# Half steps of 18-wide attention, spread over each segment of a recurrence

## The chip, the cores and the metric

The kernel runs on one core of one Trainium2 chip. TensorE multiplies matrices into PSUM; ScalarE, VectorE and POOL work beside it, each on its own list of instructions in a fixed order; SP and POOL issue transfers. The metric is the device time of one launch in microseconds, the median of the runs shown.

## The reference

Two attentions over the same `x` (2048 x 576) are mixed by a gate:

```python
def _A_ref(x, mem0, Wq, Wk, Wv, Wo, seg_len):      # H = 32 heads of 128, M = 8, seg_len = 32
    mem = mem0
    for s in range(n_seg):                          # 64 segments, one after the other
        h = concatenate([mem, xs], axis=1)          # 8 + 32 = 40 rows
        q, k, v = h @ Wq, h @ Wk, h @ Wv            # 576 -> 32 heads x 128
        p = softmax(where(mask, q k^T * scale, -1e9))
        o = (p v) Wo
        mem = o[:, :M, :]                           # carried to the next segment
        outs.append(o[:, M:, :])

def _B_ref(x, wqkv, wo):                            # 32 heads of 18, all 2048 rows, no mask
    ...
    p = softmax(q k^T * scale)
    return (p v) @ wo

return g * a + (1 - g) * b                          # g = sigmoid(sum(x * gate_w))
```

## The kernel before, in words

A first part (to about 270 us) transposes `x`, projects q, k and v of the 18-wide attention B for all rows into DRAM (`qtd`, `ktd`, `vgd`, four heads per group of 32 rows each, the rows beyond 18 being zero), and projects ahead the last 8 rows of every segment of A. Then the recurrence A runs through its 64 segments, and B is laid into it as filler. A last part mixes both and writes the output.

One step of B is one block of 128 keys against 512 queries, for the four heads of a group: four score matmuls `sb` (L330; two heads share one tile of two PSUM banks, and there are two such tiles), two exponentials `etb` on ScalarE (L342) and four matmuls of values `ob` (L346). There are 8 groups x 4 query blocks x 16 key blocks = 512 steps, written as a generator `b_steps` that `b_advance(k)` moves on by k steps. After 16 steps VectorE turns and divides `ob` (L360 to L371) and SP stores it. A new group loads `qtg`, `ktg` and `vgi` on POOL's queue into single buffers.

One segment of A: `project` (L449) multiplies the 32 rows in `ht` with half of wq, wk or wv, twenty matmuls of 512 columns, four at a time in four column strips of the array; VectorE copies the result to `tm` (L474). `turn` (L462, L465) transposes q and k with eight matmuls each into `qt` and `kt`; v goes by four transfers from `tm` into `v_sb` (L480). Then, for two halves `b` of the heads: `psh` scores (L490), exponential `et` (L498), mask by a minimum (L500); and again for two halves: sums `pss` (L508), reciprocals `rq`, broadcast `prb` (L518), product (L526), values `pso` (L531), copy to `ot` (L539). The output projection `pbw` (L547) is 160 matmuls of 128 rows, 128 columns and 40 moving columns; its first 8 columns go into the next segment's `ht` (L558 to L560).

The code writes 8 steps of B behind each segment. A scheduler decides each engine's order from the dependences and the order in the code, when the kernel is built; the lists are then fixed. Before, it moves most of the steps of one segment into the next one's first projections and softmax, seven or nine of them per segment; none stand within `pbw`. The names `sb`, `ob`, `etb` belong to B, the others to A.

## Time and profile before

| what | value |
|---|---|
| median of 3 runs | 2172.97 us (2172.16 to 2174.61) |
| the profiled execution | 2173.49 us, span 2171.8 us |
| mean granted TensorE clock | 0.857 |
| TensorE busy | 1924.1 us, 89% |
| ScalarE busy | 1087.5 us, 50% |
| VectorE busy | 822.1 us, 38% |
| DMA, mean | 54 GB/s |

A line of groups reads: line, engine, operation, output and inputs, shapes, count, busy time and mean ns of one, then the idle time of its engine ahead of it and what ended that. A line of the timeline reads: start, length, engine, line, operation and count; lengths of matmuls are those of records that overlap one another, so what one costs is read from start to start. A line of stretches gives the busy time of each engine between two points of the span, and the clock that TensorE was granted in it.

### The profile page before, as it was taken

The page shows a single profiled execution, that of the slowest core. Times are in us where ns is not written, and L with a number is a line of the kernel's source. Part 1 is how long each engine was busy: PE and PEld are TensorE (multiplying, and loading weights), DVE is VectorE, ACT ScalarE, POOL GpSimd, SP SyncE. Part 2 cuts the span into 40 slices and gives each one's busy share as a digit, 9 for nine tenths or more (in the row PEclk, how much of TensorE's full clock was granted, in tenths as well). Part 3 has the DMA queues.
Part 4 walks back from the last instruction along what each step waited for, and adds up shares of the span by engine and source line. Part 5 has one row for each costly group of instructions (what it writes and reads, how often), then busy time and mean ns, then how long its engine had stood idle before and what let it go on. Part 6 is the DMA issues. An engine that isn't in the chain of part 4 may idle for free.

```text
span 2171.8 us, 67407 instructions
## 1 busy us (share of the span) xinstructions
PE 1924.1 (89%) x30629; PEld 1083.2 (50%) x30646; DVE 822.1 (38%) x1867; ACT 1087.5 (50%) x1282; POOL 106.4 (5%) x268
## 2 busy tenths in 40 slices
PE   4799979998999899989998999989998999899986
PEld 2358735554455455554454555555544555455443
DVE  4223323333333333443433333334343333333444
ACT  2122255555555555546555555545555555555540
POOL 3000000000000000000000000000000000000000
PEclk8899978888888888888888888888888888888889
DMA  8553240001000100010001000010001000100015
GB/s 257 227 139 110 119 157 25 24 25 53 24 24 24 47 25 24 25 50 28 21 27 40 25 25 24 26 53 25 24 25 48 21 24 25 53 21 21 24 43 153
DMA packets 110291, 117.27 MB, mean 54 GB/s; under 512 B 56108, under 2 KB 91636, under 8 KB 106932
## 3 DMA queue, kind: packets, MB, share of 16 engines
q1 hardware_dynamic: 85652, 90.50, 13.4%
q10 hardware_dynamic: 20896, 9.87, 1.9%
q0 software_dynamic: 3456, 12.58, 1.8%
q8 instruction: 240, 3.93, 0.7%
q14 instruction: 47, 0.39, 0.1%
HBM read 58.91 MB, written 37.22 MB: 44 GB/s over the span
## 4 chain that ended last, share of the span: by engine, by line
PE 58%; ACT 23%; issue 7%; DMA 7%; DVE 4%; SPq 1%; ACTq 0%; POOL 0%; DVEq 0%
ACT etb L342 21%; PE pbw L547 15%; PE pvv L449 11%; PE sb L330 7%; PE ob L346 5%; PE pq L284 3%; PE pso L531 3%; PE pq L218 3%; PE prb L518 3%; PE pt L462 2%; DMA v_sb<-tm 2%; PE pq L268 2%; PE pss L508 1%; DVE et L526 1%; DMA otn<-otd 1%
## 5 line engine op out<-in xcount | busy, mean ns | idle before, releaser
L342 ACT ACTIVATE etb<-sb 128x1024 bf16<-128x1024 f32 x1024 | 990.1, 1027 | 813.9 <-PE sb L330 806.3
L474 DVE CAST tm<-pvv 128x512 bf16<-128x512 f32 x384 | 265.7, 692 | 530.3 <-PE pvv L449 530.3
L330 PE MATMUL sb<-qtg,ktg 18*128 18x512 bf16 x2048 | 404.4, 428 | 44.4 <-ACT etb L342 29.9
L547 PE MATMUL pbw<-ot,wo 128*128 128x40 bf16 x10240 | 326.6, 195 | 0.8 <-issue 0.8
L547 PEld LDWEIGHTS <-wo 128*128 128x128 bf16 x10240 | 320.0, 108 | 4.1 <-issue 0.9
L346 PE MATMUL ob<-etb,vgi 128*32 128x512 bf16 x2048 | 246.5, 425 | 53.7 <-ACT etb L342 43.1
L449 PEld LDWEIGHTS <-ht 128*32 128x32 bf16 x7680 | 185.5, 96 | 213.1 <-issue 70.9
L449 PE MATMUL pvv<-wq_m,ht 128*32 128x512 bf16 x2048 | 205.3, 388 | 0.0
L330 PEld LDWEIGHTS <-ktg 18*128 18x128 bf16 x2048 | 90.1, 92 | 223.7 <-issue 198.6
L346 PEld LDWEIGHTS <-vgi 128*32 128x32 bf16 x2048 | 95.2, 95 | 188.0 <-issue 158.3
L449 PE MATMUL pvv<-wk_m,ht 128*32 128x512 bf16 x2048 | 169.2, 380 | 0.0
L539 DVE CAST ot<-pso 128x320 bf16<-128x320 f32 x256 | 114.4, 487 | 91.8 <-PE pso L531 91.7
L449 PE MATMUL pvv<-wv_m,ht 128*32 128x512 bf16 x2048 | 133.3, 380 | 0.0
L558 DVE CAST ht<-pbw 128x32 bf16<-128x32 f32 x63 | 12.1, 192 | 271.1 <-PE pbw L547 271.1
L531 PEld LDWEIGHTS <-v_sb 64*128 64x128 bf16 x2048 | 65.3, 105 | 71.0 <-issue 57.3
L526 DVE TENSOR_TENSOR et<-et,prb 128x320 bf16<-128x320 bf16 x128 | 62.3, 487 | 97.0 <-PE prb L518 97.0
L418 POOL COPY ht<-xg 128x144 bf16<-128x144 bf16 x64 | 19.8, 310 | 1567.7 <-PE pvv L449 1567.7
L531 PE MATMUL pso<-et,v_sb 64*128 64x40 bf16 x2048 | 75.6, 196 | 23.6 <-DVE et L526 12.0
L218 PE MATMUL pq<-xT,wpk 128*128 128x512 bf16 x313 | 76.4, 405 | 18.4 <-ACT stg L228 16.1
L500 DVE TENSOR_TENSOR et<-et,cap 128x320 bf16<-128x320 bf16 x128 | 42.3, 331 | 122.0 <-ACT et L498 121.9
L490 PE MATMUL psh<-qt,kt 128*64 128x40 bf16 x2048 | 56.9, 189 | 33.6 <-DVE kt L465 33.6
L518 PE MATMUL prb<-ident,rq 128*64 128x128 bf16 (+1 forms) x768 | 71.5, 272 | 16.3 <-DVE rq L514 16.3
(103 smaller groups left out, 1524.5 us busy)
## 6 DMA issues: line engine op xcount, KB each, us to landing
v_sb<-tm SPq DMA_DIRECT2D x256, 64.0 KB
wo<-in_A_Wo_dram SPq DMA_DIRECT2D x4, 1152.0 KB
wv_m<-in_A_Wv_dram SPq DMA_DIRECT2D x4, 1024.0 KB
wq_m<-in_A_Wq_dram SPq DMA_DIRECT2D x4, 1024.0 KB
wk_m<-in_A_Wk_dram SPq DMA_DIRECT2D x4, 1024.0 KB
qtd<-stg SPq DMA_DIRECT2D x8, 512.0 KB
ktd<-stg SPq DMA_DIRECT2D x8, 512.0 KB
vgd<-vt ACTq DMA_DIRECT2D x16, 256.0 KB
```

The source lines that it names most:

```text
L218: nc.tensor.matmul(pq[:, :], lhsT=wpk[:, c, :, :].rearrange("p j e -> p (j e)"), rhs=xT[:, c, t * QC:(t + 1) * QC], start=(c == 0), stop=( ...
L284: nc.tensor.matmul(pv[:, o:o + P], lhsT=lw, rhs=xL[:, cc, q * P:(q + 1) * P], start=(c == 0), stop=(c == NF),)
L330: nc.tensor.matmul(sb[:, i, :], lhsT=ktg[32 * j:32 * j + DhB, kb * P:(kb + 1) * P], rhs=qtg[32 * j:32 * j + DhB, qc * QC:(qc + 1) * QC], s ...
L342: nc.scalar.activation(out=etb[:, :, :], in_=sbs[jp][:, :, :], func=ACT.Exp, scale=scale_b)
L346: mm = nc.tensor.matmul(ob[32 * j:32 * j + 32, :], lhsT=vg[:, kb * P + 32 * j:kb * P + 32 * j + 32], rhs=ets[j // 2][:, j % 2, :], start=( ...
L449: nc.tensor.matmul(pv[32 * j:32 * j + 32, :], lhsT=ht[:, cc, :], rhs=rw, start=(c == 0), stop=(c == NF), tile_position=(0, 32 * j),)
L474: nc.vector.tensor_copy(out=tm[:, hf * 512:(hf + 1) * 512], in_=pv[:, :])
L518: nc.tensor.matmul(prb[64 * jj:64 * jj + 64, o:o + n], lhsT=rq[0:n, 2 * k + jj:2 * k + jj + 1].to_broadcast([n, 64]), rhs=ident[0:n, 0:n], ...
L526: nc.vector.tensor_tensor(out=et[:, b, :], in0=et[:, b, :], in1=prb[:, 0:W8], op=ALU.mult)
L531: nc.tensor.matmul(pso[:, i * L:(i + 1) * L], lhsT=v_sb[64 * jj:64 * jj + 64, b * 1024 + i * Dh:b * 1024 + (i + 1) * Dh], rhs=et[64 * jj:6 ...
L539: nc.vector.tensor_copy(out=ot[:, j * HG:(j + 1) * HG, :].rearrange("p h t -> p (h t)"), in_=pso[:, 0:W8])
L547: nc.tensor.matmul(pbw[:, c * L:(c + 1) * L], lhsT=wo[:, h, d0:d0 + P], rhs=ot[:, h, :], start=(h == heads[0] and c == 0), stop=(h == head ...
```

## The change

A step of B is cut in two. A half step computes the two scores and the exponential of one pair of heads; the values of the block before are multiplied behind the first half (`values(kb - 1, before)`), so that they come one half step or more after their exponentials. The score operands take all 32 rows of a head's strip instead of 18; the added rows are zero. The 1024 half steps are given out by `tick`, sixteen times per segment (after each of the six projections, after each half of the scores, after the product and after the values of each half, and four times within the output projection), each time 0.98 of a half step on average. v is projected in two parts cut by half `b`, the first ahead of `psh`, the second behind it; each part needs four transfers of half the width.

```diff
-                for kb in range(NKB):
-                    sbs = []
...
-                                lhsT=ktg[32 * j:32 * j + DhB, kb * P:(kb + 1) * P],
-                                rhs=qtg[32 * j:32 * j + DhB, qc * QC:(qc + 1) * QC],
...
+                before = None
+                for kb in range(NKB):
+                    ets = []
+                    for jp in range(2):
+                        sb = ps_bs.tile([P, 2, QC], FP32, name="sb")
+                        for i in range(2):
+                            j = 2 * jp + i
+                            nc.tensor.matmul(
+                                sb[:, i, :],
+                                lhsT=ktg[32 * j:32 * j + 32, kb * P:(kb + 1) * P],
+                                rhs=qtg[32 * j:32 * j + 32, qc * QC:(qc + 1) * QC],
...
+                        etb = bint3.tile([P, 2, QC], BF16, name="etb")
+                        nc.scalar.activation(out=etb[:, :, :], in_=sb[:, :, :], func=ACT.Exp, scale=scale_b)
+                        ets.append(etb)
+                        if jp == 0 and before is not None:
+                            values(kb - 1, before)
+                        yield
+                    before = ets
+                values(NKB - 1, before)
...
-    per_seg = int(round(total_steps / (n_seg + 1)))
+    pace = [0.0]
+    per_tick = total_steps / (n_seg + 1) / 16
+
+    def tick():
+        pace[0] += per_tick
+        k = int(pace[0])
+        pace[0] -= k
+        b_advance(k)
...
+            tm = seg2.tile([P, 512], BF16, name="tm", bufs=6)
+            nc.vector.tensor_copy(out=tm[:, :], in_=pv[:, :])
+            tick()
+            return tm
...
+        def project_v(b):
+
+            tm = project(wv, [(2 * jj + b) * 1024 + u * 512 for jj in range(2) for u in range(2)])
+            for jj in range(2):
+                for u in range(2):
+                    nc.sync.dma_start(
+                        out=v_sb[64 * jj:64 * jj + CT, b * 1024 + u * 512:b * 1024 + (u + 1) * 512],
+                        in_=tm[64 * jj + 32 * u:64 * jj + 32 * u + CT, :],
+                    )
+
+        tq2 = [project(wq, [j * 1024 + hf * 512 for j in range(4)]) for hf in range(2)]
+        tk2 = [project(wk, [j * 1024 + hf * 512 for j in range(4)]) for hf in range(2)]
+        turn(tq2, qt)
+        turn(tk2, kt3)
+        project_v(0)
...
+            tick()
+        project_v(1)
...
+            if heads.index(h) % 8 == 7:
+                tick()
...
-        b_advance(per_seg)
```

What the built order makes of it, at three places. First TensorE at the end of an output projection before: its last matmul, values and scores of B, all 160 matmuls of `pbw` having gone ahead of them.

```order
L547 LDWEIGHTS wo
L547 MATMUL pbw<-ot,wo 128x40
L346 LDWEIGHTS vgi
L346 MATMUL ob<-etb,vgi 32x512
L330 LDWEIGHTS ktg
L330 MATMUL sb<-qtg,ktg 128x512
```

The same engine a quarter into an output projection of the changed kernel:

```order
L569 LDWEIGHTS wo
L569 MATMUL pbw<-ot,wo 128x40
L347 LDWEIGHTS ktg
L347 MATMUL sb<-qtg,ktg 128x512 [waits Activation_49]
L347 LDWEIGHTS ktg
L347 MATMUL sb<-qtg,ktg 128x512
L328 LDWEIGHTS vgi
L328 MATMUL ob<-etb,vgi 32x512 [waits Activation_49]
```

Forty matmuls of `pbw` now stand between a pair of scores and the next, and values of B follow every second pair.

Second, ScalarE around the two exponentials `et` of one segment's own scores, before:

```order
L342 ACTIVATE etb_20373<-sb_20368 128x1024
L342 ACTIVATE etb_20837<-sb_20831 128x1024
L342 ACTIVATE etb_20839<-sb_20834 128x1024
L498 ACTIVATE et_2858<-psh_20549 128x320
L498 ACTIVATE et_2858<-psh_20568 128x320
L342 ACTIVATE etb_20867<-sb_20861 128x1024
L342 ACTIVATE etb_20869<-sb_20864 128x1024
```

and changed:

```order
L356 ACTIVATE etb_20722<-sb_20719 128x1024
L516 ACTIVATE et_2858<-psh_20728 128x320
L356 ACTIVATE etb_20750<-sb_20747 128x1024
L516 ACTIVATE et_2858<-psh_20756 128x320
L356 ACTIVATE etb_20778<-sb_20775 128x1024
L356 ACTIVATE etb_20806<-sb_20803 128x1024
L356 ACTIVATE etb_20834<-sb_20831 128x1024
```

Before, five exponentials of B go ahead of both `et` in a row; now one `etb` stands between the two, and TensorE has the scores of `psh` in pieces around a pair.

Third, SP's queue over one segment, before (v in four transfers from one `tm`, between the loads of rows projected ahead):

```order
L480 DMA v_sb_2856<-tm_21068 32x1024 x4
L438 DMA xl_22079<-qld_85 128x256
L438 DMA xl_22082<-kld_86 128x256
L432 DMA v_sb_2856<-vld_84 8x2048 x2
L416 DMA xg_24873<-xtd_79 128x768
L480 DMA v_sb_2856<-tm_21622 32x1024 x4
```

and changed:

```order
L492 DMA v_sb_2856<-tm_20155 32x512 x4
L451 DMA xl_21135<-qld_85 128x256
L451 DMA xl_21138<-kld_86 128x256
L492 DMA v_sb_2856<-tm_20239 32x512 x4
L445 DMA v_sb_2856<-vld_84 8x2048 x2
L492 DMA v_sb_2856<-tm_20717 32x512 x4
```

v now leaves in two groups of four, and the loads of `xl` for the next segment stand between them.

## The prediction

> **What bounds the kernel now.** I read the page first, then the stretches of single segments, then the order of instructions inside one segment, and last the granted clock in short steps.

> ```profile
> PE 1924.1 (89%) x30629; PEld 1083.2 (50%) x30646; DVE 822.1 (38%) x1867; ACT 1087.5 (50%) x1282; POOL 106.4 (5%) x268
> L342 ACT ACTIVATE etb<-sb 128x1024 bf16<-128x1024 f32 x1024 | 990.1, 1027 | 813.9 <-PE sb L330 806.3
> ...
> PE psh L490 <- DVE kt L465: 33.6, 64, 0.5
> PE sb L330 <- ACT etb L342: 29.9, 89, 1.2
> PE pso L531 <- DMA v_sb<-tm: 9.7, 7, 2.4
> ```

> TensorE is busy for 89% of the span; ScalarE, whose exponentials (L342) take 990.1/1024 = 0.97 us each, is half idle. The three rows of waits show that little of TensorE's time is idle in the trace's own sense. Next come stretches from one write of the new memory into `ht` (L558) to the next: 62 segments together, then four single ones.

> ```profile
> 315.10:2091.57 1776.47, 1613.29 (x27480) 891.34 (x27479) 684.63 (x1628) 992.34 (x1116) 76.78 (x206) 0.85 0.10 29
> ...
> 1005.09:1033.93 28.84, 26.49 (x451) 14.27 (x450) 11.77 (x28) 17.85 (x20) 1.05 (x3) 0.88 0.11 30
> 1033.93:1060.59 26.66, 24.61 (x438) 13.84 (x434) 9.98 (x25) 14.03 (x16) 1.06 (x3) 0.87 0.08 19
> 1060.59:1090.37 29.78, 27.51 (x451) 14.72 (x450) 11.77 (x29) 17.96 (x20) 1.06 (x3) 0.83 0.08 22
> ...
> 1173.45:1203.56 30.11, 24.21 (x435) 13.98 (x434) 12.22 (x29) 13.97 (x16) 2.74 (x6) 0.83 0.25 74
> ```

> Behind the length stand the busy times of TensorE, its weight loads, VectorE, ScalarE and POOL, then the granted clock, the DMA share and GB/s. A segment costs 1776.47/62 = 28.65 us, and 64 of them make the time. The first and third hold the same work (17.9 us of ScalarE, nine 18-wide steps) and differ only in clock, 0.88 against 0.83. Where that clock goes, the next rows show, in steps of 3.41 us:

> ```profile
> 1017.99:1021.40 3.41, 2.71 (x58) 1.63 (x51) 1.58 (x3) 1.82 (x2) 0.69 (x3) 1.00 0.29 85
> 1021.40:1024.81 3.41, 2.68 (x24) 1.05 (x24) 2.89 (x9) 3.11 (x6) 0.37 (x2) 1.00 0.33 88
> 1024.81:1028.23 3.42, 3.34 (x37) 1.54 (x35) 1.49 (x6) 2.46 (x3) 0.00 (x0) 0.50 0.14 43
> 1028.23:1031.64 3.41, 3.37 (x96) 3.11 (x94) 1.18 (x3) 1.94 (x2) 0.00 (x0) 0.50 0.06 19
> 1031.64:1035.05 3.41, 3.41 (x106) 2.57 (x104) 0.85 (x4) 0.46 (x1) 0.00 (x0) 1.00 0.02 5
> ...
> 284.12:287.53 3.41, 3.41 (x24) 0.74 (x26) 0.00 (x0) 2.32 (x4) 0.00 (x0) 0.50 1.08 390
> 287.53:290.95 3.42, 3.42 (x34) 0.97 (x26) 0.69 (x1) 2.14 (x3) 0.00 (x0) 0.50 1.09 392
> 290.95:294.36 3.41, 3.13 (x40) 1.03 (x36) 0.69 (x1) 3.40 (x4) 0.00 (x0) 1.00 0.67 225
> ```

> **The change, part by part.** The costs of single visits on TensorE at full clock (second column: us):

> ```profile
> 1012.48 0.39 PE L346 MATMUL ob<-etb,vgi 128*32 128x512 bf16 x4
> 1012.80 0.39 PE L330 MATMUL sb<-qtg,ktg 18*128 18x512 bf16 x2
> 1013.12 0.83 PE L449 MATMUL pvv<-wk_m,ht 128*32 128x512 bf16 x11
> ...
> 1014.30 0.40 PE L346 MATMUL ob<-etb,vgi 128*32 128x512 bf16 x4
> 1014.52 1.04 PE L449 MATMUL pvv<-wk_m,ht 128*32 128x512 bf16 x14
> ...
> 1016.26 1.05 PE L449 MATMUL pvv<-wv_m,ht 128*32 128x512 bf16 x16
> 1018.54 0.62 PE L462 MATMUL pt<-ident,tm 128*128 128x128 bf16 x8
> ...
> 1020.01 0.89 PE L490 MATMUL psh<-qt,kt 128*64 128x40 bf16 x32 [0.53 <-DVE kt L465]
> 1020.83 0.39 PE L330 MATMUL sb<-qtg,ktg 18*128 18x512 bf16 x2
> ...
> 1049.88 0.32 PE L508 MATMUL pss<-bsel,et 128*128 128x2 bf16 x3
> 1050.48 0.45 PE L518 MATMUL prb<-ident,rq 128*64 128x128 bf16 x6 [0.28 <-DVE rq L514]
> 1050.86 0.39 PE L330 MATMUL sb<-qtg,ktg 18*128 18x512 bf16 x2
> 1051.51 0.48 PE L531 MATMUL pso<-et,v_sb 64*128 64x40 bf16 x16 [0.27 <-DVE et L526]
> 1051.92 0.33 PE L508 MATMUL pss<-bsel,et 128*128 128x2 bf16 x3
> ```

> From start to start: two projections 1016.26 to 1018.54, so 1.14 each; eight transposes 0.55; `psh` x32 0.82; a pair of scores 0.32; values ahead of a projection 0.22 (1014.30 to 1014.52), ahead of another kind 0.32 (1012.48); `prb` 0.38; `pso` x16 0.41, taken as 0.5; `pss` about 0.3. Sums to their broadcast (`pss` to `prb`, through VectorE) take 0.60, broadcast to `pso` 1.03. Then the output projection, the exponential's delay, and one VectorE step at the end of a query block:

> ```profile
> 1032.00:1033.80 1.80, 1.80 (x76) 1.79 (x72) 1.00 0.05 9
> 1056.00:1058.00 2.00, 2.00 (x66) 2.00 (x63) 0.50 0.16 41
> ...
> 1005.31 0.39 PE L330 MATMUL sb<-qtg,ktg 18*128 18x512 bf16 x4
> 1005.74 8.51 ACT L342 ACTIVATE etb<-sb 128x1024 bf16<-128x1024 f32 x9 [5.98 <-PE sb L330]
> 1006.81 0.40 PE L346 MATMUL ob<-etb,vgi 128*32 128x512 bf16 x4 [0.36 <-ACT etb L342]
> ...
> L364 DVE TENSOR_TENSOR tn<-tq,rtb 128x512 bf16<-128x512 f32 x32 | 22.4, 700 | 1.1
> ```

> Records of 0.195 us overlap the ends of a stretch, so a `pbw` matmul takes (1.80 + 0.195)/76 = 0.026 us at full clock and 0.033 at half. From the start of a score pair to the values that need its exponential: 1.50 us; exponentials in a row: 8.51/9 = 0.95.

> Now one segment of the changed order, at full clock, on TensorE:
> 1. Four projections (q, q, k, k) with four score pairs and two visits of values: 4 x 1.14 + 4 x 0.32 + 2 x 0.22 = 6.3; sixteen transposes 1.1. Sum 7.4. No exponential is late: pairs stand 1.5 us apart.
> 2. First half of v 1.14, `psh` in three pieces 0.82 + 0.2, four score pairs 1.3, values 0.33, second half of v 1.14: 4.95. The wait for `kt` (33.6 us in all) is gone, since v's first half lies over VectorE's two copies. The second v half covers the exponentials of `psh`.
> 3. The softmax: work of five score pairs, three visits of values, two each of `pss`, `prb`, `pso`, about 5.0; and three waits. Values wait 0.3: the exponential of the pair ahead of v's second half queues behind `psh`'s two and ends 0.6 into this stretch, behind a pair of 0.32. The first `pso` waits 0.3: 1.03 less `prb` and a pair. Later a pair at 3.75 has its values no earlier than 5.25, where a pair and `prb` end at 4.5: 0.75. Behind the waiting values stands the chain's own `pso`, so all three are paid: 6.35.
> 4. Output projection 160 x 0.026 = 4.2, four switches 0.4, four pairs 1.3, two values 0.65: 6.5. The copies to `ht` lie under the last pair and values.

> That is 25.2 us. What comes on top: the transposes of every fourth segment 0.1; VectorE's four instructions at the end of a query block, of 0.70 us each (L364), one of them in the chain's way in a third of the segments, 0.2; the seven changes of head group, 3.4 us each in the rows (30.11 against 26.66 with equal ScalarE time), 0.35 per segment, kept as it is, since a new group's first scores still wait for its loads. So 25.85 without the clock, against 28.65 - 2.5 = 26.15 before. The spreading takes away waits for exponentials and the clump of scores, and pays in visits: the orders have 2112 and 2650 changes between kinds of matmul with different rows and columns of the array. Each costs 0.32 - 0.22 = 0.1 us by the rows above; 538 more are 54 us, already in the walk.

> [...] Were it the whole rest of a record (0.39 - 0.22 = 0.17 us), the sum would be 37 us higher; the rows show 0.1.

> The clock: stretch 3 is as thin as the step at 1021.40 (4 visits of 512 columns and short matmuls per 3.41 us), and at 6.35 us it is nearly two grid steps long, so a step falls inside it in every segment and the clock still halves. It should return in the output projection, which now follows at once: mostly two steps (6.8 us), at times three or one; I take 7.2 us, at 0.29 us each 2.1. Segment: 27.95, and 28.65 - 27.95 = 0.7 us x 64 = 45 us gained. The end loses some 2 us, because the last score steps now run beside the last segment and their values are turned and stored after it. 2173.5 (the profiled execution; the median of the three runs shown is 2173.0) - 45 + 2 = 2130 us.

> Bounds: stretch 3 lies between its work alone, 5.0, and 7.8 (every wait twice as long); half clock between one step (1.0 us) and three (3.0). Edits that I cost at nothing: scores with 32 rows, since 18-row and 128-row matmuls of 512 columns have the same 0.39 us above (a gain is excluded too: columns set the time); score tiles allocated one by one, with two buffers as before; POOL's copy into the next `ht`, which waits for the last projection as before and is needed a segment later. The v transfers double from four to eight per segment, and this row prices the four:

> ```profile
> 1019.46 2.42 SPq L480 DMA_DIRECT2D v_sb<-tm  x4
> ```

> 0.6 us of issue each: the first half's are out 3 us ahead of its `pso`; the second half's stand behind the two loads of `xl` in SP's queue (which nobody needs before the next segment) and are out some 1.3 us ahead. Where the queue was late before, TensorE waited (9.7 us in 7 times). Cover gone costs 0.5 us per segment, 32 us; I take 0.

> **Rivals.**
> *The clock stays low through the output projection.* At half clock the new mixture (40 `pbw`, a pair, 40 `pbw`, a pair, values) has a third of its time in pairs that fill little of the array. Before, `pbw` in a block brought the clock back in the steady part; at the start, a step with 24 matmul records of projections, scores and values did not (284.12), one with 34 did (287.53, then 1.00). If the mixture falls short, half clock lasts into the next segment's projections: some 4 us of softmax, 9 of output projection (160 x 0.033 and six visits of 0.55), 2.5 of projection, 15.5 us: 8.3 x 0.29 = 2.4 us x 64, 2130 + 154 = 2284. It decides if the mixture, a third of whose time is pairs, counts for less than a step like that at 287.53.
> *The clock never drops.* [...] With the thin stretch filled by pairs and values, the step at 1021.40 might no longer occur: 2130 - 2.1 x 64 = 1996. Against it: five pairs and three visits of values in 6.35 us are no denser than what stood there before.
> *The spread buys nothing.* Exponentials and v transfers become the wait in stretch 3, where eight pairs stand within 8 us (7.6 us of exponentials, and those of `psh`): 0.6 to 1.2 us more per segment, 2168 to 2207. For it: ScalarE was busy 3.11 of 3.41 us there before. Against it: it is idle elsewhere, and no queue builds up. That the spread isn't there is excluded by the order above.

> **Numbers.** Forecast 0.51 (its own range 2070 to 2168), clock low longer 0.20, clock never low 0.07, nothing bought 0.22. No change means within 0.2%, 4 us, about what a measurement tells: 0.05, from the last case, which leaves 0.17 of it slower. Faster 0.58, slower 0.37. The range 2060 to 2275 leaves out the full-clock case and half of the low-clock one.

> **What would show it.** After: a mean segment near 28.0 us with ScalarE near 16 us in every one instead of 14 and 18; `psh` without a wait for `kt`; one low stretch of the clock per segment, of two grid steps, ending inside the `pbw` rows; waits of `pso` on `et` and of `ob` on exponentials of 0.3 to 0.8 us. A clock under 0.8 over the segments, or waits of `pso` on `v_sb` in most of them, would make the forecast wrong.

## Result and the profile after

The changed kernel takes 2076.5 us (median of 4 runs, 2072.8 to 2082.6) against 2172.6 us of the kernel before: a ratio of 0.956 [0.954, 0.959], 96 us less. The prediction was 2130 us: the direction was right and the time lies within the range, but the gain is more than twice the 43 us forecast. One execution of one kernel below, the one with all three edits together, took 2273.1 us at a mean clock of 0.648; its figures are those of the other three.

The page of the changed kernel, rows of engines and granted clock, and from the groups the exponentials:

```profile
PE 1929.8 (93%) x30629; PEld 1081.4 (52%) x30646; DVE 831.7 (40%) x1867; ACT 1119.7 (54%) x1282; POOL 107.0 (5%) x268
PEclk9899988888888888888888899888889988888999
...
L356 ACT ACTIVATE etb<-sb 128x1024 bf16<-128x1024 f32 x1024 | 1029.9, 1026 | 690.4 <-PE sb L347 689.2
```

TensorE is busy for as long as before (1924.1 us), so nearly all that went is time in which it stood still; the clock is only a little higher (0.874 against 0.857 in the profiled executions). Stretches, with the same columns as before: 62 segments from first projection to first projection, then two single segments.

```profile
318.73:1991.54 1672.81, 1610.64 (x27423) 887.57 (x27425) 693.64 (x1629) 1009.82 (x1102) 77.42 (x206) 0.87 0.11 31
1105.82:1132.73 26.91, 26.02 (x442) 14.55 (x434) 9.68 (x22) 16.45 (x18) 1.05 (x3) 0.81 0.07 19
1216.92:1242.30 25.38, 25.13 (x443) 13.82 (x443) 9.97 (x25) 16.52 (x19) 1.05 (x3) 0.93 0.08 20
```

A segment costs 1672.81/62 = 26.98 us instead of 28.65, and ScalarE has 1009.82/62 = 16.3 us in it. Not in every one, as the prediction's last paragraph had it: in about half of the segments it is within 0.2 us of 16.5, in the others it lies between 13.6 and 18.5; before, it was 13.2 to 15.0 or 16.9 to 19.0. TensorE's waits:

```profile
PE ob L328 <- ACT etb L356: 21.8, 43, 0.6
...
PE sb L347 <- DMA ktg<-ktd: 11.2, 4, 7.1
...
PE pso L552 <- DVE et L546: 8.0, 25, 0.9
...
PE pso L552 <- DMA v_sb<-tm: 5.9, 15, 0.9
PE sb L347 <- ACT etb L356: 4.9, 13, 1.2
...
PE psh L508 <- DVE kt L483: 0.2, 1, 0.2
```

The wait for `kt` is gone (33.6 us before), and the waits for exponentials and for `et` are 21.8 + 8.0 + 4.9 = 34.7 us in 81 places, half a microsecond per segment. In the kernel before they were 85.0 us in 227 places: the 29.9 for `sb` that the prediction shows, and these two:

```profile
PE ob L346 <- ACT etb L342: 43.1, 114, 0.7
...
PE pso L531 <- DVE et L526: 12.0, 24, 1.0
```

The segment at 1105.82 of the changed kernel shows such waits, in the order of TensorE's work in its softmax:

```profile
1119.91 0.39 PE L347 MATMUL sb<-qtg,ktg 32*128 32x512 bf16 x2
1120.56 0.48 PE L552 MATMUL pso<-et,v_sb 64*128 64x40 bf16 x16 [0.26 <-DVE et L546]
1120.97 0.40 PE L328 MATMUL ob<-etb,vgi 128*32 128x512 bf16 x4
...
1121.98 0.45 PE L538 MATMUL prb<-ident,rq 128*64 128x128 bf16 x6
1123.06 0.61 PE L328 MATMUL ob<-etb,vgi 128*32 128x512 bf16 x3 [0.63 <-ACT etb L356]
```

and the segment at 1216.92 has none in the same places, because its values stand elsewhere among the half steps:

```profile
1230.57 0.45 PE L538 MATMUL prb<-ident,rq 128*64 128x128 bf16 x6
1231.12 0.40 PE L328 MATMUL ob<-etb,vgi 128*32 128x512 bf16 x4
1231.45 0.39 PE L347 MATMUL sb<-qtg,ktg 32*128 32x512 bf16 x1
1231.76 0.49 PE L552 MATMUL pso<-et,v_sb 64*128 64x40 bf16 x16
...
1233.20 0.45 PE L538 MATMUL prb<-ident,rq 128*64 128x128 bf16 x6
1233.68 0.40 PE L328 MATMUL ob<-etb,vgi 128*32 128x512 bf16 x4
1234.01 0.39 PE L347 MATMUL sb<-qtg,ktg 32*128 32x512 bf16 x2
1234.33 0.56 PE L552 MATMUL pso<-et,v_sb 64*128 64x40 bf16 x16
```

The clock in its 3.41-us steps, through the segment at 1105.82:

```profile
1112.07:1115.49 3.42, 3.42 (x62) 2.07 (x60) 2.48 (x4) 1.48 (x2) 0.00 (x0) 1.00 0.00 0
1115.49:1118.90 3.41, 3.41 (x51) 1.49 (x50) 1.18 (x3) 3.21 (x6) 1.05 (x3) 1.00 0.16 42
1118.90:1122.31 3.41, 3.15 (x50) 1.86 (x46) 1.91 (x8) 3.02 (x4) 0.00 (x0) 1.00 0.22 60
1122.31:1125.73 3.42, 2.79 (x54) 1.85 (x55) 1.38 (x3) 1.61 (x2) 0.00 (x0) 0.50 0.12 37
1125.73:1129.14 3.41, 3.41 (x62) 2.05 (x59) 0.00 (x0) 1.35 (x2) 0.00 (x0) 0.50 0.02 5
1129.14:1132.55 3.41, 3.41 (x86) 2.88 (x82) 0.00 (x0) 1.72 (x2) 0.00 (x0) 0.50 0.00 0
```

It halves behind the softmax's step, as before, and here returns after the third step, at the end of the output projection. Of the 62 segments 28 have two steps at half clock, 19 three, 11 one, two four and two none.

Stages tell more than one segment. Each row of this table is a mean over the 62 segments of one profiled execution: the stages run from the first `pvv` of q to the first `pt`, to the first `psh`, to the first `pss`, to the first `pbw`, and to the next segment. "Half" is the time at half clock, (1 - mean clock) x 2 x segment, with the clock of the stretch in hundredths, so good to some 0.3 us; "at full" is the segment less 0.3 us for each us at half clock, a price that the prediction took as 0.29 and that the last experiments give as 0.33 to 0.35. In the text a score pair is two score matmuls of B, a visit of values the four matmuls `ob` of one step.

| kernel | time us | segment | project | turn, v | pairs | softmax | out | half | at full |
|---|---|---|---|---|---|---|---|---|---|
| before | 2172.6 | 28.65 | 9.59 | 4.30 | 2.27 | 6.54 | 5.95 | 8.6 | 26.1 |
| before, 32 rows | 2164.6 | 28.54 | 9.59 | 4.30 | 2.27 | 6.46 | 5.92 | 8.0 | 26.1 |
| whole steps at the end | 2132.1 | 27.86 | 10.35 | 2.78 | 2.36 | 6.43 | 5.94 | 5.6 | 26.2 |
| half steps at the end | 2119.6 | 27.61 | 10.11 | 2.86 | 2.33 | 6.62 | 5.70 | 5.0 | 26.1 |
| **changed** | 2076.5 | 26.98 | 6.53 | 2.68 | 3.81 | 5.91 | 8.06 | 7.0 | 24.9 |
| changed, 18 rows | 2101.2 | 27.31 | 6.66 | 2.68 | 3.82 | 5.92 | 8.22 | 8.2 | 24.9 |
| changed, v together | 2095.8 | 27.31 | 6.52 | 4.30 | 1.95 | 6.44 | 8.11 | 9.3 | 24.5 |
| changed, whole steps | 2126.5 | 27.75 | 6.69 | 3.00 | 3.92 | 6.25 | 7.90 | 6.7 | 25.8 |
| none in `pbw` | 2060.4 | 26.74 | 7.98 | 3.12 | 3.80 | 6.02 | 5.82 | 5.4 | 25.1 |
| none in `pbw`, half of it early | 2005.8 | 25.79 | 8.01 | 3.12 | 3.80 | 3.99 | 6.87 | 3.1 | 24.9 |
| changed, two buffers | 2055.9 | 26.60 | 6.45 | 2.68 | 3.83 | 5.72 | 7.92 | 6.9 | 24.5 |
| changed, values later | 1988.1 | 25.46 | 6.47 | 2.68 | 3.62 | 5.80 | 6.87 | 3.6 | 24.4 |
| changed, 4 matmuls added | 2117.0 | 27.63 | 6.56 | 2.68 | 3.85 | 6.57 | 7.97 | 6.6 | 25.6 |
| changed, 8 matmuls added | 2039.1 | 26.31 | 6.64 | 2.68 | 3.81 | 6.18 | 7.01 | 1.1 | 26.0 |
| early half and two buffers | 1979.9 | 25.44 | 8.06 | 3.12 | 3.82 | 3.75 | 6.69 | 2.5 | 24.7 |
| these and values later | 1913.1 | 24.22 | 7.73 | 2.72 | 3.60 | 3.96 | 6.21 | 1.0 | 23.9 |

Before to changed, TensorE's idle time ahead of its matmuls falls from 2.64 to 1.00 us per segment, which is nearly the whole 1.67: 0.70 to 0.03 in the projections, 0.92 to 0.02 in the two stages from the turns to the first `pss` (the `kt` wait and exponentials), 0.94 to 0.78 in the softmax. The stages change by more than that, because work of B moved between them. The projections lose 3.06 us: they hold 3.8 score pairs and 2.0 visits of values instead of 6.5 and 4.7, which at the prediction's prices is some 1.5 us of work that now stands elsewhere; with the 0.67 of idle time that leaves some 0.9 unaccounted for. The turns lose 1.62 (the `kt` wait, and v's second half that left this stage), the softmax 0.63; the stage named pairs gets v's second half and a score pair more (+1.54) and the output projection its half steps (+2.11). In the first three stages the changed kernel's clock is 1.00 in all segments but one; the half clock lies in the last two.

### The profile page after: what moved, and what is told of

The parts are those of the page before. It is cut to its first block, busy times and chain, and to the rows that moved or that the text cites. A ratio compares the mean times of both kernels' runs of the same rounds, so it can differ in the third digit from the quotient of the medians.

```text
span 2074.6 us, 67963 instructions
## 1 busy us (share of the span) xinstructions
PE 1929.8 (93%) x30629; PEld 1081.4 (52%) x30646; DVE 831.7 (40%) x1867; ACT 1119.7 (54%) x1282; POOL 107.0 (5%) x268
## 3 DMA queue, kind: packets, MB, share of 16 engines
q1 hardware_dynamic: 97940, 90.51, 13.9%
## 4 chain that ended last, share of the span: by engine, by line
PE 81%; DMA 9%; ACT 4%; DVE 3%; SPq 1%; issue 1%; POOL 0%; ACTq 0%; DVEq 0%
PE pvv L462 21%; PE pbw L569 16%; PE sb L347 15%; PE ob L328 9%; ACT etb L356 4%; PE pq L284 3%; PE psh L508 3%; PE pq L218 3%; PE pt L478 3%; DMA v_sb<-tm 3%; PE pso L552 2%; PE pq L268 2%; SPq L492 1%; PE prb L538 1%; DMA otn<-otd 1%
## 5 line engine op out<-in xcount | busy, mean ns | idle before, releaser
L356 ACT ACTIVATE etb<-sb 128x1024 bf16<-128x1024 f32 x1024 | 1029.9, 1026 | 690.4 <-PE sb L347 689.2
L347 PE MATMUL sb<-qtg,ktg 32*128 32x512 bf16 x2048 | 436.8, 423 | 16.4 <-DMA ktg<-ktd 11.2
L569 PE MATMUL pbw<-ot,wo 128*128 128x40 bf16 x10240 | 355.7, 194 | 0.0
L462 PEld LDWEIGHTS <-ht 128*32 128x32 bf16 x7680 | 187.5, 96 | 191.3 <-issue 49.6
L328 PE MATMUL ob<-etb,vgi 128*32 128x512 bf16 x2048 | 243.9, 433 | 25.7 <-ACT etb L356 21.8
L347 PEld LDWEIGHTS <-ktg 32*128 32x128 bf16 x2048 | 99.9, 92 | 222.9 <-issue 192.1
L462 PE MATMUL pvv<-wv_m,ht 128*32 128x512 bf16 x2048 | 147.4, 382 | 0.0
L462 PE MATMUL pvv<-wq_m,ht 128*32 128x512 bf16 x2048 | 138.6, 385 | 1.4 <-DVE ht L582 0.3
L328 PEld LDWEIGHTS <-vgi 128*32 128x32 bf16 x2048 | 69.8, 94 | 127.1 <-issue 111.2
L462 PE MATMUL pvv<-wk_m,ht 128*32 128x512 bf16 x2048 | 134.6, 380 | 0.0
L454 POOL COPY qt<-xl 128x256 bf16<-128x256 bf16 x64 | 26.2, 410 | 1484.1 <-PE psh L508 1403.8
L518 DVE TENSOR_TENSOR et<-et,cap 128x320 bf16<-128x320 bf16 x128 | 42.0, 329 | 114.7 <-ACT et L516 114.6
L508 PEld LDWEIGHTS <-kt 128*64 128x64 bf16 x2048 | 64.3, 111 | 35.8 <-issue 34.7
L508 PE MATMUL psh<-qt,kt 128*64 128x40 bf16 x2048 | 80.0, 189 | 0.2 <-DVE kt L483 0.2
```

The costliest lines, as they stand in the source:

```text
L328: mm = nc.tensor.matmul(ob[32 * j:32 * j + 32, :], lhsT=vg[:, kb * P + 32 * j:kb * P + 32 * j + 32], rhs=ets[j // 2][:, j % 2, :], start=( ...
L347: nc.tensor.matmul(sb[:, i, :], lhsT=ktg[32 * j:32 * j + 32, kb * P:(kb + 1) * P], rhs=qtg[32 * j:32 * j + 32, qc * QC:(qc + 1) * QC], sta ...
L356: nc.scalar.activation(out=etb[:, :, :], in_=sb[:, :, :], func=ACT.Exp, scale=scale_b)
L462: nc.tensor.matmul(pv[32 * j:32 * j + 32, :], lhsT=ht[:, cc, :], rhs=rw, start=(c == 0), stop=(c == NF), tile_position=(0, 32 * j),)
L508: nc.tensor.matmul(psh[64 * jj:64 * jj + 64, i * L:(i + 1) * L], lhsT=kt[:, h * L:h * L + 64], rhs=qt[:, h, :], start=True, stop=True, til ...
L569: nc.tensor.matmul(pbw[:, c * L:(c + 1) * L], lhsT=wo[:, h, d0:d0 + P], rhs=ot[:, h, :], start=(h == heads[0] and c == 0), stop=(h == head ...
```

## Experiments

**Rows of the scores.** Theory at the start: rows cost and bring nothing.

```diff
-lhsT=ktg[32 * j:32 * j + 32, ...], rhs=qtg[32 * j:32 * j + 32, ...]
+lhsT=ktg[32 * j:32 * j + DhB, ...], rhs=qtg[32 * j:32 * j + DhB, ...]
```

> The changed kernel with 18 rows per score matmul again. Theory (the gain is the place of the score steps; a matmul of 512 columns costs the same with 18 and 32 rows): 2076 us within 5, the same clock, 0.87. Rival (the clock counts filled rows, and the 14 added rows keep it up): a mean clock of 0.85 or less and 2100 us or more.

Measured: 2101.2 us, 0.969 [0.966, 0.971] of before, so 25 us above the changed kernel, with TensorE's matmuls in the same order throughout. The stages up to the softmax differ by 0.14 us at most; the time at half clock is 8.2 us per segment instead of 7.0. The rival's time and clock hold: 0.849 to 0.860 in the four runs, against 0.868 to 0.882 with the fourteen rows of zeros. In the kernel before, the same edit the other way:

> The kernel before with one edit: its score matmuls read all 32 rows of the query and key tiles, 14 of them zeros; order and placing are before's. Theory (the clock goes by how much of the array is filled, also with zeros; in the changed kernel 18 rows instead of 32 cost 25 us of 2,076): here too the half clock per segment falls from 8.6 us, mean clock over 0.857, time 2,140 to 2,163 us. Rival (rows count only where the steps lie spread between thin matmuls; in before they stand in one block of nine with the clock high): 2,166 to 2,178 us, clock 0.85 to 0.86.

2164.6 us, 0.998 [0.997, 0.999]: half clock 8.6 to 8.0, 5 us gained. The sign is that of the first edit; the size lies between the two expectations.

**Values of A.** Both halves of the v projection ahead of the pairs:

```diff
         project_v(0)
+        project_v(1)
...
-        project_v(1)
```

> The changed kernel with both halves of v projected ahead of the scores of a segment; all ticks stay. Theory (spreading the steps makes most of the gain; v's second half only fills part of the softmax): 0.3 to 1.0 us more per segment, 2095 to 2140 us. Rival (v behind the scores is what pays): 2150 us or more.

2095.8 us, 0.965 [0.963, 0.967], 19 us slower. The stage lengths at full clock are not longer (24.5); half clock is, 9.3 us. So this order pays by the clock: the softmax's stage has a mean clock of 0.73 instead of 0.84. That v's second half fills the step in which the softmax begins would explain it, and was not tested by itself. The time is at the lower end of the theory's range.

**Whole steps, spread.** Ticks give out two half steps at a time:

```diff
-        k = int(pace[0])
+        k = 2 * int(pace[0] / 2)
```

> The changed kernel with the half steps given out two at a time, eight times per segment. Theory (the spread over the segment counts, not its grain): 2065 to 2105 us, since fewer switches make up for values that wait for their exponentials. Rival (the half step is what pays): 2130 us or more.

2126.5 us, 0.980 [0.978, 0.982], 50 us slower than the changed kernel, near the rival. The half clock is not longer (6.7); the walk at full clock is, 25.8 against 24.9. Values again wait for exponentials, five times as long in all:

```profile
PE ob L328 <- ACT etb L356: 109.2, 296, 1.1
```

**No half steps in the output projection.** A second tick behind each projection of q and k instead:

```diff
+            if w is not wv:
+                tick()
...
-            if heads.index(h) % 8 == 7:
-                tick()
```

> The changed kernel with the four ticks of the output projection moved to the four projections of q and k. Theory (before, TensorE queued behind ScalarE's row of exponentials in the projections, and the gain comes from steps laid into the output projection): the first stage, 6.5 us per segment now, grows by 2 us or more, while the output projection shrinks by about 2 less the idle ScalarE: 2120 to 2180 us. Rival (the gain comes from the softmax stretch): 2100 us or less.

2060.4 us, 0.949 [0.946, 0.952], 16 us faster than the changed kernel. The theory fell: the steps inside the output projection don't bring the gain, they cost (as against a second tick in the projections). The length at full clock is about the same (25.1), but with `pbw` in one block 5.4 us are at half clock instead of 7.0. Waits for exponentials are longer than in the changed kernel:

```profile
PE ob L328 <- ACT etb L356: 56.1, 135, 0.7
```

**Everything at the segment's end.** The changed kernel with ticks only counted, and all of their half steps given out behind the output projection; then the same with the whole steps of before:

```diff
     def tick():
         pace[0] += per_tick
-        k = int(pace[0])
-        pace[0] -= k
-        b_advance(k)
...
+        k = int(pace[0])
+        pace[0] -= k
+        b_advance(k)
     b_advance(1 << 30)
```

> The changed kernel with all of a segment's half steps at its end, behind the output projection, as before placed its whole steps; half steps, 32 rows, order of the values and one key/value half per transfer stay. Theory (spreading carries most of the gain: the block of exponentials, about 16 half steps at 1.03 us, holds up the pairs and the TensorE behind it): 2,125 to 2,175 us, with the wait for the exponentials in front of the next segment's projections back and the length of projections plus steps 2 us up. Rival (half steps, rows and the moved values carry it, the spread little): 2,100 us or less.

> The kernel with everything at the segment's end (2,120 us) once more, with the steps whole as in the kernel before; rows 32 and the moved values stay. Against the kernel before with 32 rows (2,165 us) it has the moved values alone. Theory (the moved values carry nearly all of those 45 us: the wait for kt, 0.5 us a segment, and the chain from pairs to sums, which the second half of the values now covers): 2,112 to 2,138 us, stage from the turns to the pairs near 2.9 us instead of 4.3 and the next still 2.3. Rival (the half step pays here as it did when spread, 50 us): 2,148 to 2,170 us.

Half steps at the end: 2119.6 us, 0.977 [0.975, 0.979]. Whole steps at the end: 2132.1 us, 0.984 [0.982, 0.985]. With the kernels above and before's 2169.6 us beside them, the gain comes apart, in this order of edits: rows 5, v moved and the turns put ahead of it 33 (2164.6 to 2132.1), half steps 13, spreading 43; with the steps spread, rows are worth 25 and half steps 50. The first expectation's theory named too much: spreading is the largest part, but under half. The second's has the right time and stages, but the shorter stage does not make the gain. All four kernels with steps at the end have the same length at full clock, 26.1 to 26.2: moving v takes 1.5 us from the turns and gives 0.8 back in the projections, where ScalarE works through its block. ScalarE's timeline in the kernel with half steps at the end:

```profile
1104.72 5.09 ACT L356 ACTIVATE etb<-sb 128x1024 bf16<-128x1024 f32 x5 [0.78 <-PE sb L347]
1115.27 9.43 ACT L356 ACTIVATE etb<-sb 128x1024 bf16<-128x1024 f32 x10 [5.46 <-PE sb L347]
```

Ten exponentials back to back hold up the projections, behind 5.46 us without one. What moving v saves there is half clock, 8.0 to 5.6 us. Spreading does the reverse: it takes 1.2 us off the length at full clock and adds 2 us of half clock.

**Second buffers for a head group's tiles.** Keys and values of the next group are loaded into a second buffer, queries in chunks of 512 columns, one ahead:

```diff
-            ktg = bint.tile([P, S], BF16, name="ktg")
-            nc.gpsimd.dma_start(out=ktg[:, :], in_=ktd[g])
+                if qc == 1 and g + 1 < GB:
+                    nxt = load(g + 1)          # ktg, vgi with bufs=2
+                    ...
+                nq = load_q(...)               # next 512 columns of qtg
```

> The changed kernel with a second buffer for the key and value tiles of a head group and queries loaded one 512-column chunk ahead, so that the load of the next group does not wait for the last score of the one before. Theory (each of the seven changes of group holds up TensorE by about 3.4 us, 7 x 3.4 = 24 us, and nothing else hides it): 2,048 to 2,062 us. Rival (the time comes back elsewhere, as lower clock behind a gap that is gone or as transfers that delay the values): 2,068 to 2,082 us.

2055.9 us, 0.947 [0.944, 0.951], 21 us gained of 24 expected; half clock is unchanged (6.9). The theory holds.

**Half of the output projection early.** On the kernel without half steps in it, the heads whose `ot` is ready are multiplied ahead of the second half's `pso`:

```diff
             tick()
+            if b == 1:
+                pbw = ps_a.tile([P, 512], FP32, name="pbw", tag="pb")
+                out_proj(pbw, heads[:2 * HG])
             for jj in range(2):
...
+        out_proj(pbw, heads[2 * HG:])
```

> The kernel without half steps in the output projection (measured 2,060 us), with the output projection of the first 16 of 32 heads moved ahead of the value matmuls of the second half (80 matmuls, about 2.2 us), where TensorE is else filled by a half step or waits. Theory (thin pairs and score steps in the softmax stage let the clock drop, a dense run of full-array matmuls among them brings it back; the waits there, 7.5 us for et and part of 56 us for exponentials, shrink): 2,020 to 2,050 us, clock 0.91 or more. Rival (the clock is brought back by the length of one unbroken run, and two halves are worth less than one whole; the waits that go are small): 2,060 to 2,090 us, clock 0.90 or less.

2005.8 us, 0.925 [0.923, 0.927], 55 us less than without the early half, and below the theory's range. The length at full clock moved by 0.2 us; half clock fell from 5.4 to 3.1. Most of the waits for exponentials stayed:

```profile
PE ob L328 <- ACT etb L356: 41.5, 110, 0.6
```

With the second buffers as well:

> The kernel with half of the output projection early and no half steps in it (2,006 us), with the second buffers of the head groups' tiles too, which took 21 us from the changed kernel. If both are independent: 1,983 to 1,990 us, no TensorE wait for ktg but the first. Rival (a part of the gaps at a change of head group hides in the waits or lets the clock rest): 1,993 to 2,006 us.

1979.9 us, 0.912 [0.911, 0.914]: 26 us, a little more than the 21 us on the changed kernel, so neither edit takes from the other.

**Values of B one half step later.** This takes away the waits on which the prediction's third stretch rested:

```diff
-                        if jp == 0 and before is not None:
+                        if jp == 1 and before is not None:
```

> The changed kernel with the value matmuls of a step one half step later, so that its exponentials have a whole half step more. Step of the prediction (values and the chain's pso behind them wait 1.35 us per segment for exponentials, 86 us in all): most of it goes, 2,045 us or less. Theory (the trace of the changed kernel shows 21.8 us of such waits, in 43 places): 2,060 to 2,080 us, waits of ob for exponentials under 8 us. A loss above 2,085 would mean that four exponential tiles are then too few.

1988.1 us, 0.916 [0.913, 0.919], 88 us less than the changed kernel, and far more than the theory allowed. That it is as much as the prediction's 86 us of waits is chance, since the changed kernel has only 34.7 us of them. The waits, and the 62 segments:

```profile
PE sb L347 <- ACT etb L356: 16.8, 45, 1.2
...
PE pso L552 <- DVE et L546: 2.1, 4, 0.9
PE ob L328 <- ACT etb L356: 0.7, 3, 0.3
...
315.81:1894.21 1578.40, 1529.68 (x27421) 851.10 (x27414) 694.06 (x1627) 1002.30 (x1101) 77.02 (x206) 0.93 0.11 33
```

They sum to 19.6 us instead of 34.7, so 15 us went by waits. TensorE's busy time in the 62 segments fell by 81 us (1610.64 to 1529.68) with the same matmuls: that is the clock, 3.6 us at half instead of 7.0. Did the clock stay low because of the waits, or because of what work stands in each of its steps? The next two leave the values where they are and add useless work:

```diff
             prb = ps_a.tile([P, 512], FP32, name="prb", tag="pb")
+            for i in range(4):                 # then 8
+                nc.tensor.matmul(prb[:, W8:512], lhsT=wo[:, i, 0:P],
+                                 rhs=wo[:, i, P:P + 512 - W8], start=True, stop=True)
```

> The changed kernel with added work: four matmuls of 128 x 128 weights by 192 columns into unread columns of the broadcast's tile, ahead of each of the two broadcasts of a softmax (512 in all, 0.08 us each by their columns; about 0.35 us per broadcast, 42 us in all, part of it within the wait for the reciprocals). Theory (the half clock follows from too little of the array filled in the softmax stage, at about 0.3 to 0.4 us lost for each us at half clock; denser filling takes 3 us or more of the 7.0 us per segment away): clock over 0.90, time 2,000 to 2,065 us, below the changed kernel's 2,076 although its work is longer. Rival (the clock does not go by filling, the gain of the later values was their waits): clock 0.87 to 0.88, 2,080 to 2,120 us.

> The kernel with added work once more, with eight instead of four matmuls of 192 columns ahead of each broadcast (1,024 in all; 82 us of work at 0.08 us each against the changed kernel). Counted from the traces in columns times the share of the array that a matmul fills, per clock step of 3.41 us, the changed kernel's clock halves behind steps with under some 3,000 (median 2,242) and with four added matmuls still behind such steps (median 2,566). Theory (this count decides): with eight the median of such steps comes near 2,900, so that a third or more of the half clock goes, 6.6 to 3 - 4.5 us per segment, clock 0.90 to 0.94, 2,080 to 2,135 us. Rival (the clock doesn't go by filling): clock 0.885 or less, and another 40 us longer, 2,150 to 2,170 us.

Four: 2117.0 us, 0.975 [0.972, 0.978], 41 us slower than the changed kernel, as much as the added work (in the second run eight in a row take 0.83 us and seven 0.75, so 0.08 each), as the rival had it. Eight: 2039.1 us, 0.939 [0.936, 0.942], 37 us faster than the changed kernel with 82 us more work, better than the theory's range, and against the rival. First the row of waits and the segments with four, then the same with eight:

```profile
PE pso L556 <- DVE et L550: 13.9, 50, 0.9
...
PE ob L328 <- ACT etb L356: 4.7, 12, 0.9
...
317.39:2030.23 1712.84, 1669.32 (x27919) 915.13 (x27921) 693.92 (x1629) 1023.59 (x1102) 77.01 (x206) 0.88 0.10 31
```

```profile
PE pso L556 <- DVE et L550: 15.4, 55, 0.9
...
PE ob L328 <- ACT etb L356: 3.6, 9, 1.1
...
319.43:1950.59 1631.16, 1586.67 (x28416) 902.05 (x28418) 693.26 (x1629) 1024.40 (x1102) 77.35 (x206) 0.98 0.11 32
...
1097.68:1101.09 3.41, 3.15 (x47) 2.07 (x44) 1.51 (x5) 2.27 (x3) 0.00 (x0) 1.00 0.24 65
1101.09:1104.51 3.42, 3.16 (x75) 2.17 (x72) 1.38 (x3) 2.05 (x2) 0.00 (x0) 1.00 0.08 20
```

With four, the values' waits for exponentials were nearly gone (4.7 of 21.8 us; those for `et` rose from 8.0 to 13.9) and the clock still halved; with eight the waits are about the same (3.6 and 15.4 us) and it is 0.98 instead of 0.88. So the waits don't decide it here. The last two rows are a softmax's clock step with eight added and the step behind it: TensorE is busy for 3.15 of 3.41 us, exactly as in the changed kernel's row at 1118.90, and this time the clock holds. What differs is the work in the step. Counted as columns times the share that a matmul's shape has of the largest, 128 x 128 (a score or a value counts 128, a `pbw` 40, a `pso` 20, an added matmul 192), the step at 1118.90 has some 2,600, the one at 1097.68 some 3,900. This count is the author's estimate from the shapes and times of the records: how a matmul that straddles two steps is shared out moves a step by up to 5%, and some steps near 3,000 to the other side; the line at 3,000 is laid through these traces alone. Over all steps of the recurrence, from 330 to 1815 us, those behind which the clock stayed or came (up) and halved or stayed low (down):

| kernel | full clock, under 3,000: up / down | full, 3,000 or more | half clock, under 3,000 | half, 3,000 or more |
|---|---|---|---|---|
| changed | 1 / 55 | 262 / 0 | 0 / 61 | 55 / 2 |
| 18 rows, counted as 18 | 0 / 57 | 246 / 0 | 5 / 73 | 51 / 4 |
| 18 rows, counted as 32 | 0 / 52 | 246 / 5 | 2 / 64 | 54 / 13 |
| 4 added | 4 / 45 | 281 / 3 | 1 / 52 | 47 / 3 |
| 8 added | 2 / 8 | 405 / 0 | 0 / 12 | 8 / 1 |
| values later | 25 / 41 | 307 / 0 | 4 / 22 | 37 / 0 |

In the changed kernel 3 of 436 steps lie on the wrong side of that line, and other readings of the same steps tell fewer. With the best limit for each, its full-clock steps are told wrongly once by the count, but 25 times by the columns without the share of the array, 30 times by TensorE's busy time and 32 times by the longest idle gap. In the run with 18 rows, scores counted with 18 leave 9 steps on the wrong side, counted with 32 they leave 20; the changed kernel's 3 come with all its 32 rows counted, zeros too. The count does not tell everything: with later values, 25 steps under 3,000 kept the clock, all above 2,450, and in the kernel with all three edits below it is 27, while others of that size lost it. Later values change what falls into one step; how that got them past is open.

**All three together.** Early half, second buffers, later values:

> The kernel with half of the output projection early, no half steps in it and second buffers (1,980 us), with the value matmuls one half step later, which took 88 us from the changed kernel. Theory (those 88 us were some 30 us of waits for exponentials and some 60 us of half clock that the waits brought on; of the 42.6 us of such waits left here most goes, and of the half clock, 2.5 us per segment, a part): 1,925 to 1,955 us. Rival (the early block has already taken what the later values would take): 1,970 to 1,985 us.

1913.1 us, 0.882 [0.880, 0.884], 163 us below the changed kernel and better than the theory's range: half clock is down to 1.0 us per segment.

```profile
322.51:1824.16 1501.65, 1469.18 (x27423) 815.47 (x27421) 692.23 (x1629) 986.76 (x1102) 88.58 (x227) 0.98 0.12 34
```

The same 27,423 matmul records as in the changed kernel take 1469 us of TensorE instead of 1611.

## Why the prediction was right and wrong

*The step that failed: stretch 3, the softmax, and with it the walk of 25.85 us at full clock.* The prediction had 6.35 us for it, 5.0 of work and 1.35 of waits in every segment (86 us). The trace has 5.91 us, 2.0 of them at half clock, so 5.3 at full clock by the table's price; the five segments that ran it at full clock throughout took 5.07. Two terms were too large.

The waits: 34.7 us, 0.54 per segment, so 0.81 less. The lengths of the single waits were right (0.26 and 0.63 us in the rows at 1120.56 and 1123.06, against 0.3 and 0.75), their number was not: the walk took one order of pairs and values, much like that of the segment at 1105.82, for all 64. There are 15.75 half steps per segment, so what stands in the softmax shifts from one segment to the next: 81 waits in 64 segments, 1.3 in each, where the prediction had three.

The filler: the walk has 17 score pairs in a segment (4, 4, 5 and 4), but only 15.75 half steps are given out. In the softmax the trace has 4.1 score pairs and 2.05 visits of values where the walk has five and three; the third visit stands in the stretch before it. The 1.25 pairs too many, at 0.32 us, are 0.4 us.

The 0.2 us for VectorE's steps at the end of a query block shows in no row of waits; waits for `v_sb` and for the reciprocals, 0.18 us per segment, stand in its place.

*The other stretches.* The first two, at clock 1.00, came to 6.53 + 2.68 + 3.81 = 13.02 us; the prediction had 7.4 + 4.95 = 12.35, without that visit of values (0.3) and without the 0.65 on top, which it did not place. The wait for `kt` went, as forecast. The head groups' 0.35 us were about right: second buffers took 21 us. The output projection at full clock, 6.5 forecast, took 6.7 in the 55 segments of the kernel with eight added matmuls in which it ran so, and 6.1 in 21 of the kernel with later values.

*The clock* was right in place and size: 7.2 us at half clock forecast, 7.0 measured. Its price was somewhat low: 0.29 us each forecast, 0.33 to 0.35 by the added matmuls (four to eight: 1.32 us less per segment and 8 x 0.08 = 0.64 more work, over 5.6 us of half clock: 0.35), counting all added work as paid. Single segments of the changed kernel give more, 0.43, but their waits differ too, so the price stays uncertain.

*Costed at nothing.* Transfers of v: 5.9 us of waits in 15 places, 9.7 before; right. Rows of the scores, where a gain was "excluded too: columns set the time": wrong by 25 us. The median record of a score matmul is as long with 18 rows (before) as with 32 (changed), 385 ns, but the clock of the runs with 18 is lower (0.849 to 0.860 against 0.868 to 0.882).

*The ends*: the stretch behind the last full segment grew from 2171.8 - 2092.1 = 79.7 to 2074.6 - 1991.5 = 83.1 us, 3.4 for 2 forecast. The first segment, which the means leave out, took 36.1 us for 32.5; why is open. The recurrence began 0.5 us earlier.

*The sum*: at a price of 0.34, 7.0 us at half clock cost 2.4 of the 26.98, so the segment is 24.6 at full clock, 1.25 less than the walk: the waits' 0.81 and the pairs' 0.4. The price took 0.3 back (2.4 for 2.1), so that the segment came out 27.95 - 26.98 = 0.97 us short. Over 62 segments that is 60 us, less some 6 at both ends: about the 53 us missed. So a low price hid a part of an over-long walk, which is luck.

*The rivals.* "The clock stays low" needed 15.5 us at half clock; measured 7.0. It was not far in principle: steps of the output projection with its half steps in them count some 2,900 (1125.73, still low behind it) and 3,500 (1129.14). "The clock never drops" is refuted for this change, and reached within 1.0 us per segment by others. TensorE's idle time does not tell here where the clock drops: it halves behind steps that are busy for 3.15 (1118.90) and 3.33 of 3.41 us (the last row of this document), and the longest idle gap in any step of the changed kernel behind which it halved is 1.7 us. Nor do the short waits: the run with eight added matmuls has 19.0 us of those of values for exponentials and of `pso` for `et`, the run with four 18.6, but a clock of 0.98 instead of 0.88. "The spread buys nothing" is refuted by half steps at the end against the changed kernel, 43 us. The price of the 538 more changes between kinds of matmul was not measured by itself.

## What to carry to other kernels

Before a walk through one period of an order is multiplied by the number of periods, look whether the period repeats; where filler and frame have different lengths (15.75 steps here), walk several, and price a wait by how often it occurs. Add up the filler in the walk as well: it held 17 score pairs where 15.75 are given out. Where the granted clock drops, compare the work in the step ahead of the drop with that in steps behind which it held, not idle time alone: here dense matmuls moved into the thin stretch, with later values, made TensorE's same work 142 us shorter (1469 for 1611 us), and score operands of 32 rows instead of 18, the added ones zeros, made the time 25 us shorter. With the output projection in one block instead of mixed with half steps, 5.4 us per segment were at half clock instead of 7.0.

## What the hardware showed that was not expected

- Useless matmuls made the kernel faster: 1,024 of them, 82 us of work, and 37 us less time than without, at a clock of 0.958 to 0.969 instead of 0.868 to 0.882; 512 of them cost their 41 us.
- Rows of zeros made it faster: with 32 instead of 18 rows of the score operands, the same columns and results, half clock is 7.0 instead of 8.2 us per segment, 25 us in all.
- The clock halved behind a busy step: in the one at 1231.54 of the changed kernel TensorE was busy for 3.33 of 3.41 us (some 2,300 by the count above, an estimate).

```profile
1231.54:1234.96 3.42, 3.33 (x56) 1.90 (x56) 1.74 (x7) 2.79 (x4) 0.00 (x0) 1.00 0.20 54
```
